# One batch at the start of a fused attention and mixer kernel: its features, sums and x shared anew between the engines

## The chip, the cores and the metric

The kernel runs on one core of one Trainium2 chip. The metric is the device time of one execution in microseconds. The kernel before took 268.07 us (median of 3 runs, 267.79 to 268.58). A core has five engines that work side by side and wait for each other through semaphores: TensorE (PE in the profile; PEld is its loading of weights), VectorE (DVE), ScalarE (ACT), GpSimd (POOL) and SyncE (SP, which here only issues DMAs). 16 DMA engines serve the queues of SyncE, ScalarE and POOL. Matmuls write to PSUM, which has eight banks of 512 float32 columns per partition.

## The reference

Inputs are q, k and v of shape (8 batches, 8 heads, 576 tokens, 64), and four weights: `w_tok1` (576 x 256), `w_tok2` (256 x 576), `w_ch1` (512 x 1536), `w_ch2` (1536 x 512).

```python
q_p, k_p = phi(q), phi(k)          # [relu(x)*cos(theta), relu(x)*sin(theta)]: 128 features per head
kv  = einsum('bhsf,bhsd->bhfd', k_p, v)
z   = sum(k_p, axis=2)             # key sums
num = einsum('bhsf,bhfd->bhsd', q_p, kv)
den = einsum('bhsf,bhf->bhs', q_p, z) + 1e-6
x   = num / den                    # heads side by side: (8, 576, 512)
u   = x + (relu(x^T @ w_tok1) @ w_tok2)^T
out = u + relu(u @ w_ch1) @ w_ch2
```

## The kernel before, in words

**Tiles.** The 576 tokens of a batch are four chunks of 128 (token 4p+r is in partition p of chunk r) and a tail of 64, chunk number R = 4. Tails of two batches share one tile of 128 partitions. Heads 0 to 3 are `lo_heads`, 4 to 7 `hi_heads`. All matmuls are bf16 with float32 sums.

**Stages of a batch.** `feature` makes cos and sin features of q or k from the loaded float32 tile, on VectorE or ScalarE (L251). `q_trans` turns features of q by transposes on TensorE and a copy out of PSUM (L341). `values` casts v to bf16 beside a column of ones (L271). `ksum` sums the features of k (L283), `ksum_out` copies the sums to SBUF, and `dens`/`dens_out` make the reciprocal denominators (L300, L311). `kv` and `kv_out` make the 128 x 65 matrix of each head, in two halves of four heads (L315, L334). `num_half` multiplies turned features with it and `x_out` multiplies the result with the reciprocal denominators into x (L372, L377). `tok1` and the `turned_` matmuls are the token mixing; `c_block`, `c_main` and `o_step` the channel mixing with w_ch1 and w_ch2 (L572, L560, L592).

**Order.** The program is written out by hand: each engine runs its instructions in the order in which the Python code issues them. Batch 0 goes through `first_front` (L658), the stage that the change edits. From batch 1 on, `pieces` (L475) gives each piece of the next batch's front a slot among the channel matmuls of the running batch, so TensorE always has matmuls at hand. In batch 0 there are none: `first_front` puts filler matmuls on zeros (`busy`, one bf16 matmul of 512 columns or less, L199; `busy_long`, one float32 matmul of 256 columns, which runs as two, L205) between the pieces, whose results are not read. `ORDER` = (0, 1, 2, R, 3) is the order of chunks in the token mixing.

**Loads.** At the start SyncE's queue issues q, k and v of batch 0, lower heads first (upper heads of q by ScalarE's queue), then w_tok1 and w_tok2 (L104 to L119). POOL's queue issues w_tok's tail rows, and then the four blocks of w_ch1, cast to bf16 on the way (L188); `after(w_ch1_done[0], v_done)` (L190) holds the first of them back until the load `v_done`, the lower heads of v, has landed. The loads of batch 1 (L778) wait on SyncE's queue for the second block of w_ch1. w_ch2 is loaded by POOL's queue in four blocks (L193) as pieces of batch 1's plan, between POOL's casts of batch 1's v (L490 and L491). The first out-projection matmuls of batch 0 take blocks of w_ch2 as they come (`steps`, L640 to L645).

**PSUM.** Two pools: `ps_mm` with four tiles of one bank, and `ps_at` with two tiles of two banks. `kv_ps`, `num_ps` and two of the `t_ps` rotate through `ps_at`. In `num_ps` four heads of 80 columns lie in each bank.

Of the kernel before, what the change touches and what calls it, by code (L numbers as in the profile page):

```python
# [16 lines left out]
def kernel(  # L17
# [15 lines left out]
    nc = tc.nc  # L33
# [6 lines left out]
    P = 128  # L40
# [68 lines left out]
    load_tail(ktt0, k, 0)  # L109
    v_done = load_main(vt0, v, 0, 0, HH)  # L110
    load_tail(vtt0, v, 0)
    load_main(vt0, v, 0, HH, H)
# [95 lines left out]

    def cast_tok1(mi):
        nc.scalar.copy(w_tok1[:, :, mi * P:(mi + 1) * P], w_tok1n[:, :, mi * P:(mi + 1) * P])  # L210

# [7 lines left out]
    class Front:  # L219
# [156 lines left out]

        def x_out(self, num_ps, ci, den=None, halves=(0, 2)):  # L377
            lo, hi = halves
            rows = self.rows_of(ci)
            if den is None:  # L380
                den = self.d_sb[ci][rows].rearrange("p (g j) o -> p g j o", g=2)
            nv = num_ps[rows, lo:hi, 0:HH * DP].rearrange("p g (j d) -> p g j d", d=DP)
            nc.vector.tensor_mul(  # L383
                self.x_of(ci)[rows].rearrange("p (g j d) -> p g j d", g=2, j=HH)[:, lo:hi],
                nv[:, :, :, 0:D],
                den[:, lo:hi].to_broadcast([rows.stop - rows.start, hi - lo, HH, D]))
# [163 lines left out]
    AHEAD = 3  # L550

    class Channel:
        def __init__(self, b, res, tail):
# [104 lines left out]
    def first_front(f):  # L658


        idle_ps = ps_at.tile([P, 2, 512], F32, name="idle_ps", tag="at")[:, 0, :]
        lo_heads, hi_heads = (0, HH), (HH, H)
        busy_long(idle_ps, 5)

        for j in range(2):
            f.feature("q", 3, j, lo_heads, on_act=True)
        for heads in (lo_heads, hi_heads):
            for ci in range(R):
                if (heads, ci) != (lo_heads, 3):
                    f.feature("q", ci, 0, heads)  # L670
                    f.feature("q", ci, 1, heads)
                f.q_trans(ci, heads)
                busy(idle_ps, 1)
        f.q_side(R)
        f.q_trans(R, pool=ps_at)
        busy_long(idle_ps, 1)
        for ci in range(R):
            f.feature("k", ci, 0)
            f.feature("k", ci, 1, on_act=(ci > 1))
            busy_long(idle_ps, 1)  # L680
            f.ksum(ci)
        f.k_side(R)
        f.values(R, nc.vector)
        for ci in range(R):
            f.values(ci, nc.vector, hi_heads)
        for ci in range(R - 1):
            f.values(ci, nc.scalar, lo_heads)
        f.kv(0, (0,))
        busy(idle_ps, 1)
        f.ksum(R)  # L690
        f.ksum_out()
        f.values(R - 1, nc.scalar, lo_heads)
        f.kv(1, (0,))
        f.kv(2, (0,))
# [7 lines left out]
        f.kv_out((1,), on_act=(1,))  # L702
        for ci in range(NT):
            cast_tok1(ci)
        permute_tok2(0, nc.scalar.copy)
        permute_tok2(1, nc.gpsimd.tensor_copy)
        f.new_uT()
        t_ps = {}

        def num(ci, fill=0):  # L710
            num_ps = ps_at.tile([P, 2, 512], F32, name="num_ps", tag="at")
            for g in range(2):
                f.num_half(num_ps, ci, g)
            busy(num_ps[:, 1, HH * DP:512], fill)
            f.x_out(num_ps, ci)

        num_ps = ps_at.tile([P, 2, 512], F32, name="num_ps", tag="at")
        f.num_half(num_ps, ORDER[0], 0)
        f.x_out(num_ps, ORDER[0], halves=(0, 1))
        dens = f.dens(ORDER[2:])  # L720
        f.dens_out(*dens)
        f.num_half(num_ps, ORDER[0], 1)
        f.x_out(num_ps, ORDER[0], halves=(1, 2))
        num(ORDER[1], fill=4)
        for i, ci in enumerate(ORDER):
# [127 lines left out]
```

## Time and profile before

| what | us |
|---|---|
| median of 3 runs (lowest, highest) | 268.07 (267.79, 268.58) |
| the profiled execution's own time | 268.33 |
| its span, first to last instruction | 266.6 |
| TensorE busy, over the span | 261.5 |
| VectorE, ScalarE, POOL busy | 165.3, 127.8, 13.0 |
| HBM read, written | 35.85 MB, 9.44 MB |

All views that follow are of this one execution. A row of the timeline gives start, time, engine, line, operation, tiles and count; rows of like instructions are merged, and their instructions may overlap. A row of the chain gives start, time and what the end of the kernel waited for in that stretch, followed back from the last instruction; "issue" is time in which nothing that the profile shows was waited for, and a small q behind an engine's name is its sequencer, which issues DMAs. Rows by stage are a table of busy time in each stretch: the DMA share is the mean busy share of the 16 DMA engines (packets overlap at their ends, so it can pass 1).

| stretch, us | what TensorE does | PE | DVE | ACT | POOL | DMA share |
|---|---|---|---|---|---|---|
| 0 to 5.4 | fillers, first loads | 4.20 | 2.86 | 1.80 | 4.14 | 0.62 |
| 5.4 to 10.3 | q turned | 4.68 | 4.57 | 4.43 | 0 | 1.13 |
| 10.3 to 14.2 | key sums, fillers | 3.90 | 3.54 | 3.90 | 1.48 | 1.11 |
| 14.2 to 16.4 | kv, denominators | 2.20 | 1.51 | 1.03 | 0.83 | 1.06 |
| 16.4 to 21.8 | num, token mixing | 5.32 | 4.29 | 3.27 | 1.35 | 1.09 |
| 21.8 to 25.5 | turned B, first channel matmuls | 3.70 | 1.70 | 1.17 | 0 | 1.05 |
| 25.5 to 42.5 | channel matmuls of batch 0, front of batch 1 | 16.81 | 13.56 | 13.46 | 4.01 | 1.07 |
| 42.5 to 266.6 | all the rest | 220.72 | 133.31 | 98.76 | 1.22 | 0.72 |

The granted TensorE clock is 1.000 throughout.

### The profile page before, as it was taken

The numbers are of one execution on the slowest core, as the hardware profiler recorded it, in microseconds if no ns is written. First come the engines' busy times: TensorE is split into PE (matmuls) and PEld (weight loads), VectorE is DVE, ScalarE is ACT, GpSimd is POOL, SyncE is SP. The second block draws the span as 40 slices with busy tenths as digits, with TensorE's granted clock in tenths as the row PEclk, the third lists the DMA queues.
The fourth block names the chain that finished last, engine by engine and source line by source line (L and its number), as shares of the span: only waits on it lengthen the run. The fifth ranks groups of instructions, "written<-read, shape, count | busy, mean of one in ns | idle before, by whom it ended". The sixth has DMA issues, their size and how long they took to land.

```text
span 266.6 us, 5157 instructions
## 1 busy us (share of the span) xinstructions
PE 261.5 (98%) x2061; PEld 142.7 (54%) x2061; DVE 165.3 (62%) x381; ACT 127.8 (48%) x227; POOL 13.0 (5%) x29
## 2 busy tenths in 40 slices
PE   7999999999999999999999999999999999999995
PEld 5775465465644455446644455446644455445544
DVE  6974978785665946785565946876565846720022
ACT  4963794528415461646515462546515362516400
POOL 6040140010000000000000000000000000000000
PEclk9999999999999999999999999999999999999999
DMA  7999999789899999579954989379964580180032
GB/s 221 325 293 272 331 180 222 273 197 272 182 309 314 279 193 324 156 198 264 244 189 122 290 206 350 85 181 239 255 235 118 157 121 0 53 205 1 2 94 102
DMA packets 90567, 53.68 MB, mean 201 GB/s; under 512 B 59440, under 2 KB 84528, under 8 KB 90544
## 3 DMA queue, kind: packets, MB, share of 16 engines
q1 hardware_dynamic: 88288, 49.10, 68.7%
q0 software_dynamic: 1728, 3.74, 7.2%
q10 hardware_dynamic: 528, 0.52, 0.6%
q8 instruction: 16, 0.26, 0.4%
q14 instruction: 7, 0.06, 0.1%
HBM read 35.85 MB, written 9.44 MB: 170 GB/s over the span
## 4 chain that ended last, share of the span: by engine, by line
PE 83%; DMA 13%; SPq 1%; POOL 1%; issue 0%; DVE 0%
PE o_ps L599 34%; PE c_ps L566 27%; DMA vt<-in_v_dram 7%; DMA w_ch<-in_moe_w_ch_dram 6%; PE u_ps L421 6%; PE b_ps L397 6%; PE ct_ps L586 4%; PE num_ps L374 3%; PE kv_ps L326 3%; SPq L92 1%; SPq L86 1%; POOL v_aug L281 0%; POOL w_ch L193 0%; POOL w_ch L188 0%; DVE o_sb L604 0%
## 5 line engine op out<-in xcount | busy, mean ns | idle before, releaser
L599 PE MATMUL o_ps<-w_ch,h1T 128*128 128x512 bf16 (+2 forms) x408 | 94.2, 366 | 0.2 <-DMA w_ch<-in_moe_w_ch_dram 0.2
L566 PE MATMUL c_ps<-uT,w_ch 128*128 128x512 bf16 (+2 forms) x384 | 91.5, 372 | 0.0
L570 ACT ACTIVATE h1T<-c_ps 128x512 bf16<-128x512 f32 x93 | 55.3, 598 | 60.0 <-PE c_ps L566 59.9
L599 PEld LDWEIGHTS <-h1T 128*128 128x128 bf16 x408 | 37.6, 97 | 39.8 <-issue 0.5
L566 PEld LDWEIGHTS <-w_ch 128*128 128x128 bf16 x384 | 33.6, 98 | 29.8
L604 DVE TENSOR_TENSOR o_sb<-o_ps,u_sb 128x512 f32<-128x512 f32 (+2 forms) x34 | 22.4, 659 | 29.5 <-PE o_ps L599 27.5
L424 DVE TENSOR_TENSOR u_sb<-u_ps,x_sb 128x512 f32<-128x512 f32 x32 | 21.7, 689 | 8.6 <-PE u_ps L421 8.6
L428 ACT CAST u_bf<-u_sb 128x512 bf16<-128x512 f32 x28 | 17.3, 618 | 16.5 <-DVE u_sb L424 16.4
L421 PE MATMUL u_ps<-B,w_tok 128*128 128x512 bf16 x80 | 22.4, 379 | 0.0
L402 ACT ACTIVATE B<-b_ps 128x512 bf16<-128x512 f32 (+1 forms) x9 | 4.8, 549 | 34.9 <-PE b_ps L397 34.9
L383 DVE TENSOR_TENSOR x_sb<-num_ps,den 128x512 bf16<-128x512 f32 x28 | 19.4, 691 | 1.0
L586 PEld LDWEIGHTS <-w_ch 128*128 128x128 bf16 x192 | 13.9, 98 | 8.7
L397 PE MATMUL b_ps<-x_sb,w_tok 128*128 128x512 bf16 x64 | 17.7, 379 | 0.0
L268 DVE TENSOR_SCALAR qp<-qt,cos_t 128x512 bf16<-128x512 f32 (+1 forms) x35 | 15.9, 455 | 1.8 <-DMA qt<-in_q_dram 1.8
L586 PE MATMUL ct_ps<-uT_tail,w_ch 128*128 128x128 bf16 x192 | 16.9, 219 | 0.0
L279 ACT CAST v_aug<-vt 128x512 bf16<-128x512 f32 (+1 forms) x28 | 15.7, 591 | 0.1
L268 DVE TENSOR_SCALAR qp<-qt,sin_t 128x512 bf16<-128x512 f32 (+1 forms) x34 | 15.4, 454 | 0.0
L268 DVE TENSOR_SCALAR kp<-kt,cos_t 128x512 bf16<-128x512 f32 x32 | 15.1, 478 | 0.3 <-DMA kt<-in_k_dram 0.3
L604 DVE TENSOR_TENSOR o_sb<-o_ps,u_tail 128x512 f32<-128x512 f32 x4 | 2.8, 692 | 19.0 <-PE o_ps L599 19.0
L374 PEld LDWEIGHTS <-qpT 128*128 128x128 bf16 x256 | 11.6, 98 | 4.7 <-DMA qpT<-qp 0.2
L268 DVE TENSOR_SCALAR kp<-kt,sin_t 128x512 bf16<-128x512 f32 x28 | 13.4, 480 | 0.0
L374 PE MATMUL num_ps<-kv_sb,qpT 128*128 128x65 bf16 x256 | 13.0, 193 | 0.1
(98 smaller groups left out, 226.7 us busy)
## 6 DMA issues: line engine op xcount, KB each, us to landing
out_dram<-o_sb SPq DMA_DIRECT2D x29, 256.0 KB, 2.9
kt<-in_k_dram SPq DMA_DIRECT2D x7, 1024.0 KB, 6.6
vt<-in_v_dram SPq DMA_DIRECT2D x7, 1024.0 KB, 6.7
qt<-in_q_dram SPq DMA_DIRECT2D x7, 1024.0 KB, 8.6
w_ch<-in_moe_w_ch_dram POOLq DMA_DIRECT2D x4, 384.0 KB, 9.0
out_dram<-o_sb SPq DMA_DIRECT2D x9, 128.0 KB, 2.4
qtt<-in_q_dram SPq DMA_DIRECT2D x8, 128.0 KB, 5.2
kt<-in_k_dram SPq DMA_DIRECT2D x2, 512.0 KB, 6.9
```

What stands on the lines that cost most here:

```text
L268: nc.vector.tensor_scalar(o_ap, i_ap, scalar1=w, scalar2=0.0, op0=ALU.mult, op1=ALU.max)
L374: nc.tensor.matmul(num_ps[:, g, j * DP:j * DP + D1], self.qT_of(ci, g * HH + j), self.kv_sb[g][:, j, 0:D1], start=True, stop=True)
L383: nc.vector.tensor_mul(self.x_of(ci)[rows].rearrange("p (g j d) -> p g j d", g=2, j=HH)[:, lo:hi], nv[:, :, :, 0:D], den[:, lo:hi].to_broa ...
L397: nc.tensor.matmul(self.b1_ps[mi], w, self.x_of(ci), start=(ci == self.order[0]), stop=(ci == self.order[-1]))
L421: nc.tensor.matmul(u_ps, w_tok2[:, ki, ci * P:(ci + 1) * P], self.B1[:, ki, :], start=(ki == 0), stop=(ki == NT - 1))
L424: nc.vector.tensor_add(u, u_ps[rows], self.x_of(ci)[rows])
L428: nc.scalar.copy(self.ub[:, ci, :], u)
L566: nc.tensor.matmul(c_ps[:, lo:hi], w_ch1_of[:, ki, mi // 2, mi % 2, :], uT[:, lo // P:hi // P, ki, :], start=(ki == 0), stop=(ki == NCC - 1))
L570: nc.scalar.activation(self.h1T[:, mi, :], c_ps, AF.Relu)
L586: nc.tensor.matmul(self.ct_ps[:, mi % R, :], w_ch1_of[:, ki, mi // 2, mi % 2, :], self.tail.uT[:, ki, :], start=(mi % R == 0 and ki == 0), ...
L599: nc.tensor.matmul(o_ps, h, w_ch2[:, ki, cols], start=ki == 0, stop=ki == NCH - 1)
L604: nc.vector.tensor_add(o_sb, o_ps, u)
```

## The change

All of it lies in the first batch's front and its loads.

- The hold on w_ch1 is moved: `v_done` is now the load of v's tail (tokens 512 to 575), which SyncE issues behind the lower heads of v. The order of SyncE's issues stays as it was.
- q's features: chunks 1 and 2 are made over all eight heads at once, chunks 0 and 3 in halves; the order of the pieces is 0 low and 3 low, 0 high, 1, 2, 3 high. The copy of chunk 3's turned upper heads moves from ScalarE to VectorE. Fillers between the transposes: eight `busy` go, three `busy_long` come; at the start one `busy_long` is replaced by two `busy`.
- Key sums: the filler ahead of chunk 3's sums and the one ahead of the tail's sums go; kv of chunk 1's lower heads now stands ahead of the tail's sums. The cast of chunk 3's low values of v moves from ScalarE to VectorE, ahead of the high ones.
- The copies of w_tok1 and w_tok2: of w_tok1's two halves one moves from ScalarE to POOL; of w_tok2's two halves both are on POOL now, where one was on ScalarE.
- x: for all chunks but the last of `ORDER`, `num_heads` puts six heads (`HD` = 6) into the first bank of `num_ps` and two into the second. VectorE multiplies the six, in one instruction (chunk 0 in two, four heads and two), and ScalarE the other two, one activation with a per-partition scale for each. The second pair of denominators' reciprocals now stands behind chunk 1's x on VectorE. Four `busy` fillers in chunk 1's num go.

```diff
-    v_done = load_main(vt0, v, 0, 0, HH)
-    load_tail(vtt0, v, 0)
+    load_main(vt0, v, 0, 0, HH)
+    v_done = load_tail(vtt0, v, 0)
     load_main(vt0, v, 0, HH, H)
...
+        def num_heads(self, num_ps, ci, heads):
+            for h in range(*heads):
+                g, j = divmod(h, HD)
+                nc.tensor.matmul(num_ps[:, g, j * DP:j * DP + D1], self.qT_of(ci, h),
+                                 self.kv_sb[h // HH][:, h % HH, 0:D1], start=True, stop=True)
+
+        def x_heads(self, num_ps, ci, heads):
+            lo, hi = heads
+            rows = self.rows_of(ci)
+            nv = num_ps[rows, 0, 0:HD * DP].rearrange("p (j d) -> p j d", d=DP)
+            nc.vector.tensor_mul(
+                self.x_of(ci)[rows, lo * D:hi * D].rearrange("p (j d) -> p j d", d=D),
+                nv[:, lo:hi, 0:D],
+                self.d_sb[ci][rows, lo:hi].to_broadcast([rows.stop - rows.start, hi - lo, D]))
+
+        def x_rest(self, num_ps, ci):
+            rows = self.rows_of(ci)
+            for h in range(HD, H):
+                j = (h - HD) * DP
+                nc.scalar.activation(self.x_of(ci)[rows, h * D:(h + 1) * D],
+                                     num_ps[rows, 1, j:j + D], AF.Copy,
+                                     scale=self.d_sb[ci][rows, h])
...
-        busy_long(idle_ps, 5)
-
-        for j in range(2):
-            f.feature("q", 3, j, lo_heads, on_act=True)
-        for heads in (lo_heads, hi_heads):
-            for ci in range(R):
-                if (heads, ci) != (lo_heads, 3):
-                    f.feature("q", ci, 0, heads)
-                    f.feature("q", ci, 1, heads)
-                f.q_trans(ci, heads)
-                busy(idle_ps, 1)
+        busy_long(idle_ps, 4)
+        busy(idle_ps, 2)
+        both("q", 3, lo_heads, on_act=True)
+        both("q", 0, lo_heads)
+        f.q_trans(0, lo_heads)
+        f.q_trans(3, lo_heads)
+        both("q", 0, hi_heads)
+        f.q_trans(0, hi_heads)
+        for ci in (1, 2):
+            busy_long(idle_ps, 1)
+            both("q", ci, whole)
+            f.q_trans(ci, lo_heads)
+            f.q_trans(ci, hi_heads)
+        busy_long(idle_ps, 1)
+        both("q", 3, hi_heads)
         f.q_side(R)
+        f.q_trans(3, hi_heads, eng=nc.vector)
         f.q_trans(R, pool=ps_at)
         busy_long(idle_ps, 1)
         for ci in range(R):
             f.feature("k", ci, 0)
             f.feature("k", ci, 1, on_act=(ci > 1))
-            busy_long(idle_ps, 1)
+            if ci < R - 1:
+                busy_long(idle_ps, 1)
             f.ksum(ci)
         f.k_side(R)
         f.values(R, nc.vector)
+        f.values(R - 1, nc.vector, lo_heads)
...
         f.kv(0, (0,))
-        busy(idle_ps, 1)
+        f.kv(1, (0,))
         f.ksum(R)
         f.ksum_out()
-        f.values(R - 1, nc.scalar, lo_heads)
-        f.kv(1, (0,))
         f.kv(2, (0,))
...
-        for ci in range(NT):
-            cast_tok1(ci)
-        permute_tok2(0, nc.scalar.copy)
-        permute_tok2(1, nc.gpsimd.tensor_copy)
+        cast_tok1(0, nc.scalar.copy)
+        cast_tok1(1, nc.gpsimd.tensor_copy)
+        for ki in range(NT):
+            permute_tok2(ki, nc.gpsimd.tensor_copy)
...
-        f.num_half(num_ps, ORDER[0], 0)
-        f.x_out(num_ps, ORDER[0], halves=(0, 1))
+        f.num_heads(num_ps, ORDER[0], lo_heads)
+        f.x_heads(num_ps, ORDER[0], lo_heads)
         dens = f.dens(ORDER[2:])
+        f.num_heads(num_ps, ORDER[0], hi_heads)
+        f.x_heads(num_ps, ORDER[0], (HH, HD))
+        f.x_rest(num_ps, ORDER[0])
+        num(ORDER[1])
         f.dens_out(*dens)
-        f.num_half(num_ps, ORDER[0], 1)
-        f.x_out(num_ps, ORDER[0], halves=(1, 2))
-        num(ORDER[1], fill=4)
```

`both(which, ci, heads)` makes the cos and the sin feature; `num(ci)` now calls `num_heads`, `x_heads` for six heads and `x_rest`, and for the last chunk of `ORDER` the two `num_half` and `x_out` as before.

## The prediction

> **What bounds the kernel now.** I read the page first: its busy table, its slices and its chain.
>
> ```profile
> span 266.6 us, 5157 instructions
> PE 261.5 (98%) x2061; PEld 142.7 (54%) x2061; DVE 165.3 (62%) x381; ACT 127.8 (48%) x227; POOL 13.0 (5%) x29
> PE   7999999999999999999999999999999999999995
> ...
> DMA  7999999789899999579954989379964580180032
> ...
> PE 83%; DMA 13%; SPq 1%; POOL 1%; issue 0%; DVE 0%
> ```
>
> To be seen: TensorE looks full, but the DMA engines are as full for the first six slices (40 us), and 13% of the chain is DMA. So the second view is the chain over the first 45 us.
>
> ```profile
> 3.93 8.50 DMA vt<-in_v_dram
> 12.43 0.28 issue
> 12.72 0.55 POOL w_ch L188
> 13.26 8.42 DMA w_ch<-in_moe_w_ch_dram
> ...
> 21.70 0.37 SPq L86
> ...
> 22.77 9.68 DMA vt<-in_v_dram
> ...
> 32.50 0.68 POOL v_aug L281
> ...
> 33.18 1.21 POOL w_ch L193 x2
> 34.38 0.64 POOL v_aug L281
> 35.02 7.47 DMA w_ch<-in_moe_w_ch_dram
> 42.49 0.04 issue
> 42.53 1.02 PE o_ps L599 x4
> ```
>
> No TensorE instruction before 42.53 us is on it. It runs: first half of v, w_ch1's second block (landed 21.68), SyncE's release of batch 1's loads, v of batch 1, POOL's cast of it, w_ch2's third block (landed 42.49), and the first matmul that needs that block. Third, the timeline at the two places where TensorE meets a weight block:
>
> ```profile
> 25.39 0.42 PEld L576 LDWEIGHTS <-w_ch 128*128 128x128 bf16 x3 [0.23 <-DMA w_ch<-in_moe_w_ch_dram]
> ...
> 42.53 0.81 PE L599 MATMUL o_ps<-w_ch,h1T 128*128 128x512 bf16 x3 [0.21 <-DMA w_ch<-in_moe_w_ch_dram]
> ```
>
> The last block of w_ch1 (issued 14.48, 10.9 us to landing, so 25.35) comes just as TensorE reaches it: its matmul starts at 25.50 without a gap. At 42.53 TensorE really waits: eight transposes 56 ns apart before it start from 41.77 on, so the matmul could have started at 42.16, and 0.37 us are lost. From there to 266.6 I find no other start-to-start gap above 0.2 us. So time = landing of w_ch2's third block + 0.04 + 224.1 us of TensorE.
>
> **The change part by part.** First TensorE's side, up to the channel matmuls.
>
> Query features: VectorE now issues 14 of 128x256, one each 0.262 us (5.38 to 9.06, 3.68 us); after it 6 of these and 4 of 128x512 (each 0.395 us, the spacing of the key rows): 3.15 us, so -0.52. It also gets one PSUM copy of 128x512; bounds are 0.35 (a 128x256 row) and 0.69 us (L749), and I take 0.6. It then waits, as now (0.33 us until 10.26), for the second half of k: worth nothing, and covered by that idle 0.33 plus the 0.52.
>
> ScalarE loses one of eight such copies (0.476 apart), so its sines of k start up to 0.5 earlier (now 11.76) and its casts of v at about 12.7 instead of 13.18.
>
> Key sums: the filler before chunk 3's sums (two f32 matmuls, 0.30+0.22 us) and the one before the tail's (0.22) go. The tail sums then wait for VectorE's tail feature alone (13.51) and run at 13.6 instead of 14.22; ks_sb at 13.95 instead of 14.60, the first kv_sb copy at 15.1 instead of 15.66. What is late next: the second half of v lands at 14.22 and four casts (14.25 to 15.33) follow. The second half of kv then ends some 0.3 us after 15.33+0.2, at 15.8 instead of 16.23, and x begins 0.43 earlier. The added cast of low values on VectorE (0.27 us) lies in its idle 13.84 to 14.25.
>
> x: now a chunk costs VectorE 0.61 us (rows of 0.69, overlapped by 0.08). With six heads it is 384 columns: half-way between the rows of 256 (0.39) and of 512 (0.69) lie 0.54, less the overlap 0.46. ScalarE adds two activations of 64 columns; between ks_sb (8 columns, 0.17) and kv_sb (260 columns, 0.38) that is 0.21, plus 0.08 for the scale operand: 0.5 to 0.6 us per chunk, beside VectorE. ScalarE is clear of w_tok2, as its copies left it; one w_tok1 cast (0.62) stays ahead of x and ends near 16.8, where the first x_rest's sums are ready. Chunks 1, 2 and the tail save 0.15 each: the x of chunk 3 ends at 20.53-0.43-0.45 = 19.65.
>
> POOL: the second half of w_tok1, bounds 0.73 (its v cast) to 1.11 us (L213), I take 1.1, starts behind the four w_ch1 issues (15.9) and is done at 17.0, ahead of its matmul near 17.7. Both w_tok2 halves follow: landed 18.72, then 1.11+0.29 for the first and 1.11 for the second, so 21.4. That is what ends last now: the matmuls on B (21.83 to 23.5) move up by 0.5 to 0.7, and the channel matmuls would begin at 22.9.
>
> There the gain stops. Nine matmuls later TensorE needs w_ch1's last block, landed at 25.35: of 0.6 us only 25.50-25.39 = 0.11 passes. At 42.16-0.11 it meets w_ch2's third block, landed at 42.49: the rest becomes a longer wait. TensorE's side is worth **0**, as long as the gate lies where it is.
>
> Now the DMA side, which the change touches in one place: w_ch1's issue on POOL waits for the tail of v (issued 5.77, 7.5 us, so 13.30) instead of the first half of v (12.43). The four issues move by 0.87 us, 12.72 to 13.59; behind them on POOL stand the copies above, and on SyncE batch 1's loads, which wait for w_ch1's second block. What that costs is seen in the DMA view of three stretches, 12.7 to 15.6, 15.6 to 16.5 and 16.5 to 17.7 us (packets, MB, share of the engines):
>
> ```profile
> q1 hardware_dynamic: 550, 1.17, 104.6%
> ...
> q0 software_dynamic: 40, 0.12, 68.8%
> q1 hardware_dynamic: 80, 0.15, 44.1%
> ...
> q0 software_dynamic: 87, 0.25, 104.6%
> ```
>
> q0 is POOL's queue. Though issued at 12.72, it moves nothing until 15.66; until then SyncE's queue fills the engines, and at 16.4 it is empty. Without q0 its last 44.1% of 0.9 us would be done at 16.0. So w_ch1's later issue is free if its first packet comes by 16.0, as the engines never idle and the bytes up to each gate are the same. Bounds for that packet: w_ch2 shows 1.24 us from issue (33.18) to packet (34.42), so 14.8, cost 0; w_ch1 itself shows 2.94, so 16.53, cost 0.53 us of idle engines. I take 16.1, cost **0.1**: w_ch1's is the nearest row, but a large part of it was spent behind SyncE's queue, which the later issue finds shorter.
>
> Here a rule speaks against the change. The Trainium skill, "SBUF — State Buffer", section "Who interferes with whom", says that VectorE copies in a two-port mode lock POOL out of the port through which it writes descriptors. The trace allows it: the added cast fills VectorE's gap at 13.84, so by that rule the descriptors wait until 15.33, and w_ch2's 1.24 from there gives 16.57, a cost of 0.57 in place of 0.1.
>
> Sum: 0 + 0.1. The profiled execution took 268.33 (span 266.6 and 1.73 around it), 0.26 over the median 268.07; I add the 0.1 to both: 268.4 and **268.2**. Below, a gate that lands earlier can give no more than 0.37+0.11 before TensorE's own work binds, unless its 0.6 comes through as well.
>
> **The rivals.** (1) Slower: w_ch1's whole string moves with its issue. Its 8.42 us from issue to landing stay what they are, SyncE's release, v and w_ch2 follow, and TensorE waits 0.87 longer at 42.5: 268.07+0.87 = 268.9 or more. For it: the chain has each link straight behind the last. Against: engines at 104.6% without it. It decides once the first packet comes later than 16.0, and reaches 0.3% from 16.8 on. By the skill's rule above the string would be there at 16.57.
> (2) Faster: the landings move up and TensorE's gain comes through: 0.37+0.6 = 1.0 less, 267.1. For it: SyncE's loads are alone until 16.0, so w_tok2 lands early, and the landings hang on a last engine (w_ch1's last block: 15 of 16 engines had signalled by 24.0, the last at 25.05). Against: nothing in the change takes bytes away ahead of either gate. It decides when batch 1's k is issued before 21.2.
> (3) Slower by TensorE's own side: POOL's two w_tok2 copies or its w_tok1 copy come late. The wait at 42.5 and the 0.6 cover about 1.0 us; beyond that it counts. If each of POOL's copies started only after the 2.94 us, the w_tok1 half would be ready at 18.8+1.1, 2.2 late: 268.07+1.2 = 269.3.
>
> **How the numbers follow.** Forecast 0.60 (267.6 to 268.7: the 0.49 below, the 0.53 above, both from the median), rival 1 0.19, rival 2 0.16, rival 3 0.05. 0.3% is 0.8 us, about what this kernel's three runs (267.79 to 268.58) can tell from no change. Faster is rival 2, 0.16; slower rivals 1 and 3, 0.24; same 0.60. For the range I keep 8 in 10 by leaving out rival 3, the far half of rival 2 and part of rival 1 above 269.1: 267.3 to 269.1.
>
> **What would show it.** Key sums' copy near 14.0, x of chunk 3 done near 19.65 and c_ps begun near 22.9 show TensorE's side right; a new gap of about 0.5 us near 24.8, waiting for w_ch, and a longer one at 42.2 show the gates. POOL's first packet at 16.1 or before, batch 1's first k issue near 21.8 and w_ch2's third block near 42.6 show the DMA side. I am wrong if either issue time moves by over 0.5 us, if c_ps begins after 23.6, or if the time after 42.5 is not 224.1 to 0.5 us.

## The result, and the profile after

The changed kernel took 269.39 us (median of 21 runs, 268.20 to 270.46) against 268.15 us of the kernel before (21 runs, 267.75 to 268.90): a ratio of 1.0044 (95% interval 1.0031 to 1.0058). It is slower, by 1.24 us between the medians, and lies outside the range 267.3 to 269.1. The forecast of no change was wrong. One execution of those that follow, at 272.70 us in the run without the hold, is over 1.5% above its kernel's fastest and is left out of that run's numbers.

The profiled execution took 268.98 us. Its span is 266.9 us, only 0.3 above the one shown before. The page's span, TensorE's busy time, the DMA slices and the shares of the chain:

```profile
span 266.9 us, 5122 instructions
...
PE 258.9 (97%) x2033; PEld 141.4 (53%) x2052; DVE 164.8 (62%) x379; ACT 127.4 (48%) x230; POOL 15.1 (6%) x32
...
DMA  7999998889999999279954989389974570170032
...
PE 78%; DMA 12%; DVE 4%; SPq 2%; POOL 1%; issue 1%
```

The first thing to be seen is a subtraction. 268.98 less 266.9 leaves 2.08 us outside the span, where the kernel before had 268.33 - 266.6 = 1.73. Over all executions the medians are 2.15 (2.08 to 2.20, 21 executions) and 1.77 (1.70 to 1.84, the 35 executions of the kernel before beside the first four experiments). So some 0.38 us of the 1.24 lie where no row of the page is.

The chain over the first 45 us has the links of before (start, time, what was waited for):

```profile
5.74 7.71 DMA vtt<-in_v_dram
13.45 0.28 issue
13.73 0.58 POOL w_ch L188
14.31 6.66 DMA w_ch<-in_moe_w_ch_dram
...
20.99 0.37 SPq L86
...
22.05 10.14 DMA vt<-in_v_dram
...
32.24 0.68 POOL v_aug L281
...
35.00 7.91 DMA w_ch<-in_moe_w_ch_dram
42.90 0.04 issue
42.95 0.38 PE o_ps L625
```

w_ch1 is issued 1.01 later (13.73 for 12.72), and yet its second block lands earlier: batch 1's first load is issued at 20.99 instead of 21.70. That lead is lost again in v (10.14 for 9.68 us), between the links, and in w_ch2 (7.91 for 7.47), and w_ch2's third block lands at 42.90, 0.41 later than in the execution shown before. The DMA view of the stretches 12.7 to 15.6 and 15.6 to 16.5 us says why the later issue is free (packets, MB, share of the engines):

```profile
q1 hardware_dynamic: 530, 1.18, 104.8%
...
q0 software_dynamic: 45, 0.14, 85.5%
q1 hardware_dynamic: 49, 0.08, 23.5%
```

SyncE's queue q1 fills the engines until 15.6, as before, and POOL's first packet moves at 15.60 (before 15.66).

The timeline, where x is made, has the surprise (start, time, engine, line, operation, count, and in brackets the idle time ahead and what ended it):

```profile
16.81 0.80 DVE L387 TENSOR_TENSOR x_sb<-num_ps,d_sb 128x128 bf16<-128x128 f32 x2 [0.39 <-PE num_ps L380]
17.14 1.03 ACT L396 ACTIVATE x_sb<-num_ps,d_sb 128x64 bf16<-128x64 f32 x4 [0.37 <-DVE x_sb L387]
...
17.71 0.40 PE L380 MATMUL num_ps<-kv_sb,qpT 128*128 128x65 bf16 x8 [0.69 <-DVE d_sb L312]
...
18.15 0.56 DVE L387 TENSOR_TENSOR x_sb<-num_ps,d_sb 128x384 bf16<-128x384 f32 x1
...
18.74 0.52 ACT L396 ACTIVATE x_sb<-num_ps,d_sb 128x64 bf16<-128x64 f32 x2 [0.57 <-DVE x_sb L387]
18.82 0.55 DVE L387 TENSOR_TENSOR x_tail<-num_ps,d_sb 64x384 bf16<-64x384 f32 x1
...
19.41 0.51 ACT L396 ACTIVATE x_tail<-num_ps,d_sb 64x64 bf16<-64x64 f32 x2
...
19.75 0.69 DVE L406 TENSOR_TENSOR x_sb<-num_ps,d_sb 128x512 bf16<-128x512 f32 x1 [0.38 <-PE num_ps L374]
```

ScalarE's part of a chunk doesn't run beside VectorE's part of the same chunk. It starts when that part has ended: 17.14 behind 17.10, 18.74 behind 18.71, 19.41 behind 19.37, and twice the row names VectorE's x as what ended the wait. The bank pair is free for the next chunk only when both are done, so TensorE stands idle ahead of the numerators of chunk 2 at 17.71 (0.85 us from start to start; the row puts it down to VectorE's d_sb, but the count that this raises came at 17.714, behind the matmul's start at 17.708; what had ended by then is ScalarE's x of chunk 0, at 17.66) and 0.25 us ahead of those of chunk 3. x of chunk 3 ends at 20.44, and the channel matmuls begin at 23.47, only 0.09 earlier than in the kernel before. Their rows, before and after:

```profile
23.55 2.75 PE L576 MATMUL c_ps<-uT,w_ch 128*128 128x512 bf16 x12
```

```profile
23.47 2.75 PE L602 MATMUL c_ps<-uT,w_ch 128*128 128x512 bf16 x12
```

So standing in line took away TensorE's gain in this stage; it did not make the stage longer than before.

That leaves three candidates for the time: the time outside the span, the two engines in line, and the moved hold with its gates.

### The profile page after: what moved, and what is told of

The parts are those of the page before. It is cut to its first block, busy times and chain, and to the rows that moved or that the text cites. A ratio compares the mean times of both kernels' runs of the same rounds, so it can differ in the third digit from the quotient of the medians.

```text
span 266.9 us, 5122 instructions
## 1 busy us (share of the span) xinstructions
PE 258.9 (97%) x2033; PEld 141.4 (53%) x2052; DVE 164.8 (62%) x379; ACT 127.4 (48%) x230; POOL 15.1 (6%) x32
## 4 chain that ended last, share of the span: by engine, by line
PE 78%; DMA 12%; DVE 4%; SPq 2%; POOL 1%; issue 1%
PE o_ps L625 34%; PE c_ps L592 24%; PE u_ps L444 6%; PE b_ps L420 6%; DMA w_ch<-in_moe_w_ch_dram 5%; PE ct_ps L612 4%; DMA vt<-in_v_dram 4%; DMA vtt<-in_v_dram 3%; PE kv_ps L326 3%; DVE x_sb L406 2%; PE num_ps L374 2%; SPq L86 1%; DVE den L368 1%; SPq L92 1%; DVE den L369 1%
## 5 line engine op out<-in xcount | busy, mean ns | idle before, releaser
L625 PE MATMUL o_ps<-w_ch,h1T 128*128 128x512 bf16 (+2 forms) x392 | 92.7, 366 | 1.3 <-DMA w_ch<-in_moe_w_ch_dram 0.7
L451 ACT CAST u_bf<-u_sb 128x512 bf16<-128x512 f32 x28 | 17.2, 618 | 16.7 <-DVE u_sb L447 15.1
L268 DVE TENSOR_SCALAR qp<-qt,sin_t 128x512 bf16<-128x512 f32 (+1 forms) x32 | 15.1, 473 | 0.0
L374 PEld LDWEIGHTS <-qpT 128*128 128x128 bf16 x232 | 10.6, 98 | 4.7 <-issue 0.6
L444 PEld LDWEIGHTS <-w_tok 128*128 128x128 bf16 x80 | 7.8, 98 | 9.5
```

The costliest lines, as they stand in the source:

```text
L268: nc.vector.tensor_scalar(o_ap, i_ap, scalar1=w, scalar2=0.0, op0=ALU.mult, op1=ALU.max)
L374: nc.tensor.matmul(num_ps[:, g, j * DP:j * DP + D1], self.qT_of(ci, g * HH + j), self.kv_sb[g][:, j, 0:D1], start=True, stop=True)
L444: nc.tensor.matmul(u_ps, w_tok2[:, ki, ci * P:(ci + 1) * P], self.B1[:, ki, :], start=(ki == 0), stop=(ki == NT - 1))
L451: nc.scalar.copy(self.ub[:, ci, :], u)
L625: nc.tensor.matmul(o_ps, h, w_ch2[:, ki, cols], start=ki == 0, stop=ki == NCH - 1)
```

## Experiments: the parts one by one

Each experiment ran beside the kernel before on the same chip. "Outside" is the time less the span, the median over the executions.

**The hold alone.** The kernel before, with `v_done` on the load of v's tail and nothing else:

```diff
-    v_done = load_main(vt0, v, 0, 0, HH)
-    load_tail(vtt0, v, 0)
+    load_main(vt0, v, 0, 0, HH)
+    v_done = load_tail(vtt0, v, 0)
```

> The kernel before with one edit: w_ch1's first block waits for the tail of v instead of its first half. Theory G (the gates: the end is set by when w_ch2's third block lands, and the later issue is hidden behind SyncE's queue): w_ch1's first block is issued 0.9 to 1.0 us later, its packets start where they did (15.6 to 16.0), time 0 to +0.3 us against the kernel before. Theory H (w_ch1's string moves with its issue): +0.9 to +1.2 us, the whole of the change's loss. Theory C (fewer fillers let the array's clock fall): 0, and no execution with a granted clock under 0.995.

Measured: 268.44 against 268.38 us, ratio 1.0003 (0.9993 to 1.0013); median span 266.7 against 266.6, outside 1.755. The first issue of w_ch1 was at 13.08, its first packet at 15.51. The hold costs nothing within 0.35 us.

**All but the hold.** The changed kernel with those two lines put back:

> The changed kernel with the hold on w_ch1 put back to the first half of v. Theory G: as slow as the changed kernel, +0.9 to +1.3 us against the kernel before. Theory H: back to the kernel before, within 0.3 us. Theory C: still some executions with a clock near 0.986, 1.0 us or more longer than the others.

Measured: 269.09 us, ratio 1.0031 (1.0010 to 1.0051); median span 267.0, outside 2.14. The loss is there without the hold. Three of the twelve executions had a granted clock of 0.992 to 0.994.

**The query part alone.** The kernel before, with the order of q's features, their fillers and the copy of chunk 3's upper heads from the change:

```diff
+        both("q", 3, lo_heads, on_act=True)
+        both("q", 0, lo_heads)
...
+            both("q", ci, whole)
...
+        f.q_trans(3, hi_heads, eng=nc.vector)
```

> The kernel before with the query part alone as in the change: features of two chunks over all heads, the fillers between the transposes replaced by three long ones, one copy moved to VectorE. Theory C: executions with a granted clock near 0.986 appear here (about one in five), and the median is 0.3 to 1.0 us over the kernel before. Theory G and theory H: within 0.3 us of the kernel before, all clocks above 0.995.

Measured: 268.86 us, ratio 1.0015 (1.0004 to 1.0027). Span 266.7 against 266.6, outside 2.11 against 1.77: of its 0.48 us 0.34 lie outside the span. No execution had a granted clock under 0.998, so the fillers between q's transposes alone do not bring the lower clocks of the changed kernel.

**The x part alone.** The kernel before, with six heads for VectorE and two for ScalarE, the new order of the denominators, the copies of w_tok1 and w_tok2 on POOL and without the four fillers:

```diff
+                f.num_heads(num_ps, ci, whole)
+                f.x_heads(num_ps, ci, (0, HD))
+                f.x_rest(num_ps, ci)
...
+            permute_tok2(ki, nc.gpsimd.tensor_copy)
```

> The kernel before with the last part alone as in the change: six heads' x by VectorE and two by ScalarE from a second bank, the second denominators behind chunk 1's x, one half of w_tok1 and both halves of w_tok2 copied by POOL, four fillers gone. Theory G: within 0.3 us of the kernel before, since TensorE's gain or loss here of up to 1.0 us is covered by the two waits for weight blocks. Theories H and C: the same, and clocks above 0.995. If instead it takes 0.5 us or more, the two-engine x is itself slower than that cover.

Measured: 269.07 us, ratio 1.0023 (1.0006 to 1.0040). Span 267.15, that is 0.5 more than before, and 1.91 outside, 0.14 more. This is the case that the expectation names last: the two-engine x is slower than its cover. TensorE waits 0.85 us ahead of the numerators of chunk 2, the channel matmuls begin at 23.77 instead of 23.55, and w_ch2's first matmul at 38.62 instead of 38.19; w_ch2's third block landed at 41.25 in this trace, so no gate hid or made a loss. Here it is TensorE's own side that got longer, by 0.22 us up to the channel matmuls; the trace is of the fastest of the twelve executions (268.39), so it doesn't show the whole 0.5.

What follows: hold 0, query part 0.48 (0.34 of it outside the span), x part 0.69 (0.14 of it outside). These come near the 1.24 us, but the parts outside do not simply add: the changed kernel has 0.38 there, and not 0.48. The key part, with its fillers, was not run alone.

## Experiments: two engines in line

What makes ScalarE wait? Both write x into different columns of one SBUF tile, both read `num_ps`, but different banks of it. In the recorded program the first activation of each pair waits for the count that VectorE's product raises; with an x tile of its own for ScalarE that wait stays (the program was only recorded, not run), with a PSUM tile of its own it turns into a wait for TensorE (and for chunk 2 also one for VectorE's d_sb, as the row at 17.98 below shows). So the wait goes with the shared PSUM tile; it is one that the program sets, and no run here shows that the chip would need it. The experiment puts ScalarE's two heads into a bank of the other pool:

```diff
-                nc.tensor.matmul(num_ps[:, g, j * DP:j * DP + D1], self.qT_of(ci, h),
+                nc.tensor.matmul(num_ps[g][:, j * DP:j * DP + D1], self.qT_of(ci, h),
...
+        def two_tiles():
+            a = ps_at.tile([P, 2, 512], F32, name="num_ps", tag="at")[:, 0, :]
+            return a, ps_mm.tile([P, (H - HD) * DP], F32, name="rest_ps", tag="mm")
...
+                num_ps = two_tiles()
```

> The changed kernel, but the two heads of ScalarE have a PSUM tile of their own (one bank of the pool ps_mm), so that ScalarE reads another tile than VectorE. Nothing is left out. Theory 'the two engines stand in line' (ScalarE's part of x waited for VectorE's part of the same chunk, in the changed kernel 17.137 behind 17.104 and 18.740 behind 18.706): each first ACTIVATE of L396 begins with TensorE's end and beside VectorE, VectorE's three 128x384 products follow each other with less than 0.2 us between them, TensorE's stall of 0.85 us before the numerators of chunk 2 goes, x of chunk 3 ends at 19.7 to 20.0 instead of 20.44, c_ps begins at 22.8 to 23.1 instead of 23.47, and the median span falls by 0.2 to 0.5 us, from 267.2 (0.2 where the gate of the third block of w_ch2 takes the rest). The time outside the span stays at 2.13 us. Rival 'the chunks wait for something else' (TensorE's own order, the two buffers of num_ps): c_ps stays at 23.4 to 23.5 and the span at 267.1 to 267.3.

Measured: 268.98 us against 268.08, ratio 1.0032 (1.0020 to 1.0045); median span 266.85 against 266.3, outside 2.135. The timeline of the same stretch:

```profile
16.66 0.80 DVE L387 TENSOR_TENSOR x_sb<-num_ps,d_sb 128x128 bf16<-128x128 f32 x2 [0.33 <-PE num_ps L380]
...
16.72 0.93 ACT L396 ACTIVATE x_sb<-rest_ps,d_sb 128x64 bf16<-128x64 f32 x4
...
17.98 0.52 ACT L396 ACTIVATE x_sb<-rest_ps,d_sb 128x64 bf16<-128x64 f32 x2 [0.33 <-DVE d_sb L313]
17.99 0.56 DVE L387 TENSOR_TENSOR x_sb<-num_ps,d_sb 128x384 bf16<-128x384 f32 x1
...
18.39 0.50 ACT L396 ACTIVATE x_tail<-rest_ps,d_sb 64x64 bf16<-64x64 f32 x2
18.46 0.54 DVE L387 TENSOR_TENSOR x_tail<-num_ps,d_sb 64x384 bf16<-64x384 f32 x1
...
19.04 0.69 DVE L406 TENSOR_TENSOR x_sb<-num_ps,d_sb 128x512 bf16<-128x512 f32 x1
```

The activations now start with the product or ahead of it. x of chunk 3 ends at 19.73, and the channel matmuls begin at 22.76: 0.7 earlier than in the changed kernel, and close to the 19.65 and 22.9 that the prediction had worked out for two engines side by side. But TensorE then stands at w_ch1's third and fourth blocks, which landed at 24.34 and 25.87 in this execution:

```profile
24.39 0.82 PE L602 MATMUL c_ps<-uT,w_ch 128*128 128x512 bf16 x3 [0.17 <-DMA w_ch<-in_moe_w_ch_dram]
25.91 0.82 PE L602 MATMUL c_ps<-uT,w_ch 128*128 128x512 bf16 x3 [0.70 <-DMA w_ch<-in_moe_w_ch_dram]
```

That is 0.34 + 0.86 us from start to start. The theory holds for the stage of x, and in this execution so does the prediction's step that the gates take TensorE's gain. How much the tile is worth in the time is shown further down, on one chip.

## Experiments: the time outside the span

What the kernels with more time outside have in common is VectorE's count of instructions in the trace, its semaphore instructions included:

| kernel | VectorE's instructions | outside, us (median) |
|---|---|---|
| before; the hold alone | 448; 448 | 1.77; 1.755 |
| the x part alone | 447 | 1.91 |
| the query part alone; all but the hold; own bank; changed kernel | 445 each | 2.11; 2.14; 2.135; 2.15 |

Also, a last packet of 8192 bytes on the queue of instructions starts behind the last instruction: 0.66 us behind it in the kernel before, 1.36 with 447 instructions, 1.62 in the changed kernel. The test adds memsets of one column on VectorE at the start, where it is idle from 1.16 to 1.70 us: three in the changed kernel (448), sixteen in the kernel before and nineteen in the kernel with the own bank (464 both).

```diff
+    spare = head.tile([P, 3], F32, name="spare")
+    for i in range(3):
+        nc.vector.memset(spare[:, i:i + 1], 0.0)
```

> The changed kernel with three memsets of one column on VectorE at the start (where it is idle from 1.16 to 1.70 us), so that VectorE has 448 instructions, as before the change, instead of 445. Nothing is left out. Theory 'the last block of instructions is fetched late' (the time outside the span goes by the number of VectorE's instructions: 448 gave 1.77 and 1.755 us, 447 gave 1.91, 445 gave 2.11 to 2.15): the time outside falls from 2.13 to 1.75 to 1.80 us, and the last fetch of 8192 bytes starts 0.6 to 0.9 us behind the last instruction instead of 1.63; the span stays at 267.2 and the time falls to 268.9 to 269.1. Rival 'another engine's number of instructions, or the change of the program's end': 2.10 to 2.15 outside, and a time of 269.3 to 269.5.

> The kernel before with sixteen memsets of one column on VectorE at the start: 464 instructions. Nothing is left out. Theory of the late fetch: the fetch comes ahead of the last wait and not behind it, so the time outside the span is not over 1.77 us, and 1.1 to 1.6 if 448 still waited for it; the span stays at 266.6, and the time is 267.7 to 268.3 against 268.38. Rival 'the number of instructions does not matter': 1.77 outside and the time unchanged within 0.1 us. Rival 'it is the place in the block that counts, not whether it is reached': anything from 1.7 to 2.2.

> The changed kernel with both: the two heads of ScalarE in a PSUM tile of their own, and nineteen memsets of one column on VectorE (464 instructions). Nothing is left out. If both theories hold, the two parts add: the span as in the run with the own bank (266.7 to 267.0) and the time outside as in the kernel before with 464 (1.1 to 1.77), so 267.8 to 268.8, no slower than the kernel before (268.38) within its uncertainty. If only the own bank holds: 268.8 to 269.1. If only the fetch holds: 268.3 to 269.0 with c_ps still at 23.4 to 23.5. If neither: 269.4. Executions with a granted clock of 0.986 to 0.994, of which the changed kernel had 4 of 21, may stay, since the fillers are not put back: 1 to 4 of 12.

Measured: outside 1.765, 1.815 and 1.78, so the time outside follows the count, and 464 gives no less than 448. But the times rose: 272.02 us, ratio 1.0155 (1.0115 to 1.0194); 271.51, 1.0127 (1.0109 to 1.0144); 270.37, 1.0089 (1.0076 to 1.0103). The spans were 270.25, 269.7 and 268.55. None of the expectations had that. (The trace of the kernel before with sixteen memsets is of its slowest execution, 274.35 us.) VectorE's setup was not late (its last memset ends at 4.88 in all of them), but the loads were: the second half of v landed at 14.86, 15.54 and 15.45 us, where it landed at 13.82 to 14.46 in the kernel before, the changed kernel and the one with the own bank. What the three share is the new tile in the first pool. It put q's tile at byte 16928 (three columns), 16960 (sixteen) and 16992 (nineteen) of each partition instead of 16896, which is 33 times 512, and every tile behind it as far off. So the count was tested again without a tile: the memset of `bias0` is issued four times.

```diff
-    nc.vector.memset(bias0, 0.0)
+    for _i in range(4):
+        nc.vector.memset(bias0, 0.0)
```

> The changed kernel with the memset of bias0 issued four times instead of once: 448 instructions on VectorE, and no new tile. The run with 448 before this one took its three memsets in a tile of their own in the first pool; that put the tile of q at byte 16928 instead of 16896 (33 times 512) of each partition, and every tile behind it 32 bytes further. Nothing is left out. Theory 'the late fetch goes by VectorE's count': 1.75 to 1.80 us outside the span. Theory 'the tiles' place made that run's span 270': here the tiles lie as in the changed kernel, so the span is 266.9 to 267.5 and the time 268.7 to 269.2, 0.36 under the changed kernel, and still 0.3 to 0.7 over the kernel before. Rival 'the three instructions themselves, or their place at the start, cost the 3 us': a span of 269 to 270 again.

Measured: 269.13 us against 268.38, ratio 1.0036 (1.0019 to 1.0052); span 267.35, outside 1.765. The span is that of the changed kernel again, and the time outside is that of the kernel before. The other engines' programs are those of the changed kernel, so VectorE's count alone takes 0.38 us off (2.15 less 1.765).

**Both mended.** The same, with ScalarE's two heads in their own bank:

> The changed kernel with the own PSUM tile for ScalarE's two heads, and with 448 instructions on VectorE by the repeated memset of bias0. Nothing is left out. If the two parts add: the span of the run with the own bank (before's and 0.2 to 0.5) with 1.77 us outside, so 0.2 to 0.5 over the kernel before of the same call. What is then left over is the TensorE side's gain, given back at w_ch1's last block: c_ps at 22.7 to 22.9 and waits of 0.5 to 1.2 us in all at the third and fourth blocks. If what is left is the array's clock, the executions with 1.0 alone equal the kernel before within 0.1 us.

Measured, on the same chip: 268.29 us against 268.38, ratio 1.0002 (0.9985 to 1.0019); span 266.5, outside 1.77. Against the run with the tiles shared (269.30 and 268.48 are the means of twelve) that is 0.83 us less, ratio 0.9969 (0.9948 to 0.9991). With both causes gone the change costs nothing and wins nothing, within 0.5 us. That 268.29 is the 268.2 of the forecast is in part luck: the forecast came from gates that take TensorE's gain, and in this kernel's trace none did. The expectation had the channel matmuls at 22.7 to 22.9 and waits of 0.5 to 1.2 us at w_ch1's blocks; they began at 23.30, without a wait. The profiled execution had a span of 265.8, and its chain shows what is left where the gates open early:

```profile
span 265.8 us, 5129 instructions
...
PE 90%; DVE 5%; DMA 2%; issue 1%; ACT 0%
```

w_ch1's last block landed at 25.02 and w_ch2's third at 40.76, and TensorE waited for neither.

**x as before.** The changed kernel with x by VectorE alone, the casts of the weights on their old engines and the four fillers back, and 448 instructions:

```diff
-                f.x_heads(num_ps, ci, (0, HD))
-                f.x_rest(num_ps, ci)
+            busy(num_ps[:, 1, HH * DP:512], fill)
+            f.x_out(num_ps, ci)
```

> The changed kernel with its x part undone: x of all eight heads by VectorE from one tile, the casts of w_tok1 and w_tok2 on the engines of before, the four fillers of the numerators back; the query part, the key sums ahead, and the later release of w_ch1 stay. The memset of bias0 is issued three times, so that VectorE has 448 instructions. Nothing is left out. Theory 'the span's excess is the x part standing in line': the span is that of the kernel before or up to 0.4 less (ks_sb at 14.0 to 14.2 and c_ps at 23.0 to 23.3, then the gates), 1.77 outside, and the time equal to the kernel before or up to 0.4 faster. Rival 'the query and key parts cost on their own (fillers gone, the clock)': a span 0.2 or more over the kernel before, or executions with a granted clock under 0.995.

Measured: 268.92 us, ratio 1.0015 (0.9991 to 1.0038); span 267.15, outside 1.765. The spans of its twelve executions lie between 266.2 and 268.7, and the interval holds both the theory and its rival. The two signs named for the rival came: a median span over 0.2 us longer than before (0.55), and one execution with a granted clock under 0.995 (0.993). So this run doesn't settle how much of the loss in the span is the x part's. In its trace (span 266.2) the channel matmuls begin at 23.10 and neither gate is waited for.

**The tiles' place.** The kernel before with the sixteen memsets again, but in a tile of 512 bytes instead of 64:

```diff
+    spare = head.tile([P, 128], F32, name="spare")
+    for i in range(16):
+        nc.vector.memset(spare[:, i:i + 1], 0.0)
```

> The kernel before with the sixteen memsets of one column again (464 instructions on VectorE), but their tile is 512 bytes of each partition instead of 64, so that every tile behind it lies a whole 512 bytes further (q's from byte 17408 = 34 times 512, in the kernel with the 64 bytes 16960). Nothing is left out. Theory 'the place against 512 bytes made the loads longer' (1024-byte packets of the load queue took 52 ns in the mean where the tiles lay at multiples of 512, 58 and 62 where they lay 32 and 64 off): mean 52 ns again, and a span of 266.2 to 267.0, 1.77 outside, 268.0 to 268.8 in all. Rival 'any shift of the tiles, or the sixteen instructions, cost the 3 us': 269 to 271. For the late fetch: 464 instructions give 1.75 to 1.82 us outside, no less than 448.

Measured: 268.41 us, ratio 1.0002 (0.9985 to 1.0020), span 266.65, outside 1.77. The same sixteen instructions cost nothing when the tiles lie at multiples of 512 bytes. SyncE's queue over the first 45 us, in the DMA view, first of the kernel with the 512 bytes and then of the one with the 64:

```profile
q1 hardware_dynamic: 9713, 8.05, 56.9%
```

```profile
q1 hardware_dynamic: 9344, 7.67, 64.9%
```

Fewer bytes took more of the engines' time. In the mean a packet of 1024 bytes of that queue took 50.8 ns in the first and 62.3 in the second; 58.2 with the tiles 32 bytes off, 57.9 with 96 off, 52.1 in the kernel before.

**Where the spans differ.** The traces allow a sum that the experiments above leave out. In the kernel with both causes mended TensorE took 242.50 us from its first channel matmul to the end of the span. In the ten other traces with tiles at multiples of 512 bytes, everything that comes on top of these 242.50 us comes before 103 us; behind that they agree within 0.04 us.

| kernel | channel matmuls begin, us | lost up to 58 us | lost from 58 to 103 us | span |
|---|---|---|---|---|
| before | 23.55 | 0.49 | 0.01 | 266.55 |
| changed | 23.47 | 0.88 | 0.01 | 266.85 |
| the hold alone | 23.53 | 0.12 | 0.62 | 266.76 |
| all but the hold | 23.38 | 0.01 | 0.44 | 266.33 |
| the query part alone | 23.23 | 0.95 | 0.42 | 267.10 |
| the x part alone | 23.77 | 0.22 | 0.00 | 266.49 |
| own bank | 22.76 | 1.32 | 0.14 | 266.71 |
| 448, tiles shared | 23.75 | 0.24 | 1.09 | 267.58 |
| both mended | 23.30 | 0 | 0 | 265.81 |
| x as before, 448 | 23.10 | 0.00 | 0.53 | 266.16 |
| before, tile of 512 bytes | 23.43 | 0.11 | 0.56 | 266.60 |

TensorE lost time at w_ch2's third block in three of these eleven executions only (before, changed, the query part alone). In seven it lost 0.14 to 1.09 us later, and the waits that the rows name there are for q's features of a later batch, which a DMA turns. The kernel with 448 and the tiles shared shows it most:

```profile
101.29 0.42 PE L375 MATMUL num_ps<-kv_sb,qpT 128*128 128x65 bf16 x8 [0.44 <-DMA qpT<-qp]
```

So of the 1.78 us between the traces of "448, tiles shared" and "both mended", only 0.45 lie ahead of the channel matmuls, where the tile was changed; 0.24 lie up to 58 us and 1.09 behind it, where the two programs are the same. That the tile takes time off is shown by the twelve executions of each (0.83 us, 0.25 to 1.41); where it does so is shown only for these 0.45.

## Why the prediction was wrong, step by step

- **"0.5 to 0.6 us per chunk, beside VectorE"** is the first step that failed. The size was right (two activations take 0.52, VectorE's 384 columns 0.56, forecast 0.54), the word "beside" was not. Two engines that read one PSUM tile stood in line, so a chunk took 0.56 + 0.52 us until TensorE had the banks back. x of chunk 3 ended at 20.44 instead of 19.65 and the channel matmuls began at 23.47 instead of 22.9. Against the kernel with separate tiles this costs 0.83 us in the means (0.25 to 1.41), and the x part alone had 0.5 more in the span. I had read from the code that the heads lie in two banks, and not asked for which tile the waits are kept. By the prediction's own sum this step alone makes nothing slower, for the gain that was lost had been put at 0.
- **"TensorE's side is worth 0, as long as the gate lies where it is"** is the second. Its basis, "time = landing of w_ch2's third block + 0.04 + 224.1 us of TensorE", was read from one execution in which TensorE waited at that block, and eight of the eleven traces in the table lost nothing there. It held in the own bank's trace, where the matmuls began 0.8 us earlier than before and w_ch1's blocks took it. It did not hold between the kernels with the tiles shared and apart (448 instructions both): they differ in that tile alone, and by 0.83 us in the means. Nor is TensorE's own time all that follows 42.5: seven traces wait for q's turned features behind 58 us.
- **"I add the 0.1 to both"** is the third: the sum took the 1.73 us outside the span as given. They are 2.15 now. The query part has three VectorE instructions fewer, and with 445 instead of 448 the program ends 0.38 us later behind its last instruction. This term was in no sum and no rival.
- **Key sums, kv**: ks_sb 14.11 (forecast 13.95), first kv_sb copy 15.16 (15.1), x begun 16.00 instead of 16.41, so 0.41 earlier (0.43). The PSUM copy on VectorE took 0.42, inside its bounds 0.35 to 0.69 and under the 0.6 taken. All right.
- **POOL**: the half of w_tok1 took 0.61, not 1.1, and ended at 16.68 (17.0); w_tok2's main parts ended at 19.53 instead of 21.4, since w_tok2 landed at 17.10 instead of 18.72 (the prediction's own terms add up to 21.2, not 21.4). Rival 3 didn't happen in its own form. It is the one that named TensorE's side, but by another mechanism.
- **The hold, 0.1, and rival 1**: the first packet came at 15.60, under the 16.0 from which it would have cost. The hold alone measured 1.0003. Rival 1 falls; the low end of the bounds, 0, was the right one.
- **Rival 2** said that the gain comes through if batch 1's k is issued before 21.2. It was issued at 20.99, 0.8 ahead of the 21.8 of the forecast (over the 0.5 that was named as a sign of being wrong), and the gain didn't come: 0.71 us of lead were lost in v's load, in the links behind it and in w_ch2's. One reading for it was off: of the sixteen signals of w_ch1's last block 11 had come by 24.0 us, not 15, and the last came at 25.35. The landing of w_ch2's third block was 42.49 and 42.90 in the two kernels, 41.61 with the hold alone and 40.76 with both causes mended, with no instruction of its chain behind 21 us changed. One execution's 42.49 is not the program's gate. In the trace with both causes mended, span 265.8, what this rival describes did happen: both gates opened early and TensorE's gain came through. "The time after 42.5 is 224.1" held in the changed kernel's trace: 224.0 from 42.90 on.

What stays open: why the span of the changed kernel is 0.6 us longer than before (267.2 against 266.6) though its channel matmuls begin as early. Its own trace, only 0.3 longer, puts that down to w_ch2's third block, which landed 0.41 us later; but this landing varies by 2 us over the traces. Nor is it known whether the key part, which was not run alone, costs a few tenths in the span. And 4 of the changed kernel's 21 executions had a mean granted clock of 0.986 or 0.987 and spans of 268.0 to 268.3, where of the 96 executions of the kernel before beside the experiments one was under 0.995. They are a small part of the loss: the other 17 have a median of 269.12 us. None of the four was profiled. One trace does show such a fall, that of the kernel before with sixteen memsets in 64 bytes: TensorE had nothing to do for 2.64 us until 41.01, waiting for VectorE's features of q, and from 41 to 44 us the granted clock was 0.51 (mean over the execution 0.994). Whether such a stop came in the four isn't shown. Fillers are fewer in the changed kernel, but the kernel with both causes mended has as few, and none of its 12 executions was under 0.998.

## What to carry to other kernels

When work on one PSUM tile is shared between two engines, look up what the second one waits for in the recorded program: two banks of one tile can stand in line where two tiles run side by side. Compare the time less the span, not the span alone; here three instructions more or fewer on one engine moved the end by a third of a microsecond. And a gate that is a DMA's landing has a spread between executions (here 40.76 to 42.90 us over the traces), so a sum made with one landing is good for the order of the lanes, not for tenths; ask in more than one trace whether the gate is waited for at all.

## What the runs showed of the hardware

- **The end of this program depends on VectorE's number of instructions.** 445: 2.11 to 2.15 us outside the span in four kernels; 447: 1.91; 448: 1.75 to 1.78 in six; 464: 1.77 to 1.815 in three. The last 8192-byte packet of instructions starts 1.62 to 1.65 us behind the last instruction with 445, 1.36 with 447, 0.62 to 0.89 with 448, and ahead of the end with 464. That the late packet is what makes the end wait fits these numbers; shown is only that the time outside follows the count.
- **Where a load's tile starts within 512 bytes matters.** Off by 32, 64 or 96 bytes, packets of 1024 bytes took 58, 62 and 58 ns, where they took 50 to 52 in the eleven traces with tiles at multiples of 512, and the spans were 1.7 to 3.4 us longer than those of the same kernels without the new tile; a shift by 512 bytes cost nothing. Steps between 96 and 512 were not run. The Trainium skill, "DMA: Bandwidth & Descriptors", section "How a descriptor splits into AXI transactions", says that a descriptor that does not start at a multiple of 256 bytes has its first transaction start at the boundary below, and that the bytes ahead of it still cost beats. The direction agrees; by its count of beats 1024 bytes 32 off would take 33 in place of 32, an estimate of 3%, and the trace shows 12%.
- **VectorE's casts can hold up POOL's DMA issues.** In five of the fourteen traces an issue of w_ch1 on POOL lasts until VectorE's last cast of v is done, and the next one comes 0.11 to 0.12 us behind that cast's end: casts end at 14.99 and the next issue is at 15.10, 15.29 and 15.40, 15.47 and 15.58, 14.92 and 15.03, 14.38 and 14.50 (there the issue before it had begun at 11.79). That is the rule that the prediction weighed (the Trainium skill, "SBUF — State Buffer", section "Who interferes with whom"), and these five traces agree with it. The other nine, the kernel before and the changed one among them, do not show it: no issue lasts over 1.0 us there, though they too fall among the casts (in the changed kernel the third, 14.89 to 15.50, with casts from 14.48 to 15.38). What tells the two apart isn't shown. And w_ch1's first packet does not follow the first issue: issued at 11.79, 12.46, 12.72, 13.08 and 13.73, it came at 15.38, 15.23, 15.66, 15.51 and 15.60. Until then SyncE's queue had the engines (104.8% of them in the changed kernel's view above), so a later issue hid behind it. In the two traces whose first issue was held longest into that time, the own bank's to 15.12 and the one with 448 and shared tiles to 15.42, the first packet came at 15.82 and 16.14; whether that cost a few tenths isn't shown.
